# Wo sums on GpSimd, second-wave sums moved, LN steps of neighbouring tiles swapped, w2 ending on four banks

## The chip, the cores and the metric

One core of one Trainium2 chip runs the whole program. The metric is the device time of one execution in microseconds (us), as a median of runs. Inside a profile, times are counted from the span's start.

## The reference, cut to what matters

```
x  : [2048, 1024];  six rows sa, ca, ga, sb, cb, gb = silu(c) @ w_mod
h  = layernorm(x) * (1 + ca) + sa
x1 = x + ga * A(h)                  # attention over 64 segments of 32 tokens, 8 memory tokens, 32 heads of 128
                                    # A ends with o @ Wo  (4096 x 1024)
u  = layernorm(x1) * (1 + cb) + sb
g  = gelu(layernorm(u) @ w1)        # 1024 x 1024, then four channel groups shifted by -1, +1, -2, +2 tokens
v  = u + shifted(g) @ w2
out = x1 + gb * (v + gelu(layernorm(v) @ w3) @ w4)      # 1024 x 3584 and 3584 x 1024
```

## The kernel before

Matrix products are made with one level of a Strassen-like scheme: seven products in place of eight, whose operands are sums of blocks ("sums") and whose results are joined by additions. The work comes in stages, one after the other on TensorE (PE).

**Attention** (about 110 to 773 us). A scheduler orders the instructions of each engine by their place in the program and its own estimates; `keep_order` pins an instruction to its place. Head by head, projections (L649) run between the heads' scores and outputs (L757, L774). VectorE (DVE) joins results (L621), multiplies masks (L763), makes the projection weights' sums (L592) and the sums of Wo, `wo_sum` (L569 to L575): for each of 16 blocks of 256 rows of Wo, four additions of 128x512 16-bit elements, both inputs in SBUF, and a store `WoT_d` (L576) from GpSimd's queue (POOL). Twelve blocks come from tiles `wo2` (two buffers), four from `wstream` (one buffer, shared with loads of the weight check on SyncE's queue, SP). POOL otherwise stores heads (L799) and copies their memory columns (L806 to L808).

**Output projection, two waves** (773 to 990 us). Here and in the next stage the order is written out by hand: `units` is a list of TensorE units of 8 matmuls, and `put(n, f)` places the instructions of `f` behind unit n on every engine. Wave 0 is units 0 to 55 and wave 1 is units 56 to 111. In each wave the seven products come in the order j = 1, 2, 5, 6, 3, 7, 4, each 8 units long (two halves `hf` of four token tiles). `after(j, i)` empties a bank: `snap` copies it on ScalarE (ACT, L946); `fin` adds the snap on DVE (L952) and multiplies by ga (L954). In wave 1, product j=2 is units 64 to 71, j=5 is 72 to 79, j=6 is 80 to 87, j=3 is 88 to 95, j=7 is 96 to 103, j=4 is 104 to 111. A new bank for j=5 needs the `fin` of j=2 done, and j=4 adds onto the bank that j=7's `fin` reads. The eight sums of wave 1, `sums1[hf][k]` (L1002, 128x4096 each), are put at given units.

**Layer norms of the 16 token tiles** run beside the waves and the w1 product. Tile t has a start n in `starts`; at n POOL adds the residual, `C1_x` (L1141, two halves), and issues the stores `x1_d` (L1145); at n+2 DVE takes statistics, `ln_stats` (L1125 to L1129), and POOL makes rstd (L1131, L1132); at n+3 ACT makes u (L1151); at n+5 `C1_mod` on DVE multiplies, adds and takes the second statistics (L1155, L1156, L1125), and POOL makes the second rstd; at n+8 ACT makes z (L1163); at n+9 `C1_out` issues the transposition of z (L1174) and the store of u (L1168), from ACT's queue up to tile 8, from SP's queue behind it. The load of the residual for tile t, `load_x2` (L1118), goes out on POOL's queue at max(n-9, the start of tile t-2).

**w1** (units 112 to 143, L1230): four blocks of 512 tokens of 8 units each. Blocks 2 and 3 need the transposed z of tiles up to 12 and up to 15.

**w2** (`Ba`, L1366): 16 tiles, two banks each, taken in turn from eight banks; DVE adds u (L1368), ACT squares and normalises (L1346, L1353), POOL makes rstd between them.

**w3 and w4** (L1442, L1493; order by hand again): `w3_stage` opens its own bank pools, `bank_b` (four banks), `bank_e` and `bank_d` (two each). In each group of products the copies `snap` (L1407, ACT) of `bank_b` and `bank_d` come before PE adds onto these banks, and `join` (L1450, DVE) and gelu (L1446, ACT) follow.

Of the kernel before, what the change touches and what calls it, by code (L numbers as in the profile page):

```python
# [14 lines left out]
ALU = mybir.AluOpType  # L15
# [14 lines left out]
NTT = S // P  # L30
# [30 lines left out]
def kernel(ctx, tc, A_x, A_mem0, A_Wq, A_Wk, A_Wv, A_Wo, A_seg_len, B_x, B_w1, B_w2, B_w3, B_w4, c, w_mod, out,  # L61
           dbg=None, force_fallback=False, no_fallback=False):
    nc = tc.nc
# [17 lines left out]
    x1_d = dram.tile([S, D], F32, name="x1_d")  # L81
# [70 lines left out]
    def lagged(a_fn, b_fn, ts, lag=2):  # L152
        n = len(ts)
        out_ = []
        for i in range(n + lag):
            fs = []
            if i - lag >= 0:
                fs.append(b_fn(ts[i - lag]))
            if i < n:
                fs.append(a_fn(ts[i]))  # L160
            out_.append(lambda fs=fs: [f() for f in fs])
        return out_

    def p_rows(t):

        if t == 0:
            return [(slice(0, 32), slice(0, 32)), (slice(32, 128), slice(S - 96, S))]
        return [(slice(0, P), slice(32 + P * (t - 1), 32 + P * t))]

    def first_pass(late_hook):  # L170
# [3 lines left out]
        acc_pools = [psA, psA, psX]  # L174
# [71 lines left out]
        keep_order = tc.keep_in_program_order  # L246

        keep_order = tc.keep_in_program_order
# [262 lines left out]
        def f16(ap):  # L511
            return ap.bitcast(F16)

        hA = []
        for p in range(2):
# [3 lines left out]
            s1 = nc.vector.tensor_tensor(S1, A21, A22, ALU.add)  # L519
# [40 lines left out]
        def wo_sum(k, w):  # L560

            B11, B12, B21, B22 = (w[:, b, n] for b in range(2) for n in range(2))
            st = []

            def one():
                st.append(wtp.tile([P, 2, 2, 512], BF16, name="wt"))
                T1, T3, T4, T2 = (f16(st[0][:, b, n]) for b in range(2) for n in range(2))
                st.append((T1, T2, T3, T4))
                keep_order(nc.vector.tensor_tensor(T1, B12, B11, ALU.subtract))  # L569
                nc.vector.tensor_tensor(T2, B22, T1, ALU.subtract)  # L570

            def two():
                T1, T2, T3, T4 = st[1]
                keep_order(nc.vector.tensor_tensor(T3, B22, B12, ALU.subtract))
                nc.vector.tensor_tensor(T4, B21, T2, ALU.subtract)  # L575
                nc.gpsimd.dma_start(WoT_d[:, :, k, :].rearrange("j p c -> p j c"), st[0][:].rearrange("p b n c -> p (b n) c"))  # L576
            return [one, two]

# [356 lines left out]
        x1s = {}  # L935
# [102 lines left out]
        psB = PS.enter_context(tc.tile_pool(name="psB", bufs=4, space=PSUM))  # L1038
# [75 lines left out]
        def load_x2(t):  # L1114
            if t < NTT and t not in xts2:
                xts2[t] = tp.tile([P, D], BF16, name="xt2")
                for rows, toks in p_rows(t):
                    nc.gpsimd.dma_start(xts2[t][rows, :], x2[toks, :])  # L1118
# [16 lines left out]
        def halves_of(ap):  # L1135
            return [ap[:, n * 512:(n + 1) * 512] for n in range(2)]

        def C1_x(t):
            for n in range(2):
                cs = slice(n * 512, (n + 1) * 512)  # L1140
                nc.gpsimd.tensor_tensor(x1s[t, n][:], x1s[t, n][:], xts2[t][:, cs], ALU.add)  # L1141
            for n in range(2):
                cs = slice(n * 512, (n + 1) * 512)
                for rows, toks in p_rows(t):
                    nc.gpsimd.dma_start(x1_d[toks, cs], x1s[t, n][rows, :])  # L1145

        def C1_u(t):
            nmr, rstd = ln[t]
# [4 lines left out]
        def C1_mod(t):  # L1153
            u = us[t]
            nc.vector.tensor_tensor(u[:], u[:], cb1_b[:], ALU.mult)  # L1155
            nc.vector.tensor_tensor(u[:], u[:], sb_b[:], ALU.add)  # L1156
            rstd = bsm.tile([P, 1], F32, name="ln_rstd")
            ln_stats(t, halves_of(u[:]), rstd[:])
# [28 lines left out]
        def next_a(key, hf=None):  # L1187
            def f():
                for x in range(2) if hf is None else (hf,):
                    load_a(1, key, x)  # L1190
            return f
# [47 lines left out]
        def put(n, *fs):  # L1239
            at.setdefault(n, []).extend(fs)  # L1240
# [6 lines left out]
        put(31, next_a((0, 0)))  # L1247
        put(39, next_a((1, 0)))
        put(47, next_a((1, 1)))
        for n, (hf, k) in {58: (0, 0), 60: (1, 0), 62: (0, 1), 64: (1, 1), 65: (0, 2), 67: (1, 2), 76: (0, 3), 78: (1, 3)}.items():  # L1250
            put(n, sums1[hf][k])
        put(79, load_w1)
        put(98, late_slots)
        put(111, open_h1, load_w2)
        starts = [40, 46, 51, 56, 72, 77, 82, 87, 97, 101, 105, 109, 113, 116, 119, 122]
        for t, n in enumerate(starts):
            put(max(n - 9, starts[t - 2] if t > 1 else 0), lambda t=t: load_x2(t))
            put(n, lambda t=t: C1_x(t))
            put(n + 2, lambda t=t: ln_stats(t, [x1s[t, k][:] for k in range(2)], ves[:, t:t + 1]))
            put(n + 3, lambda t=t: C1_u(t))  # L1260
            put(n + 5, lambda t=t: C1_mod(t))
            put(n + 8, lambda t=t: C1_z(t))
            put(n + 9, lambda t=t: C1_out(t))
        put(134, check_b)
# [110 lines left out]
            return lambda: nc.sync.dma_start_transpose(z2s[t // 8][:, :, t % 8 * P:(t % 8 + 1) * P], zs[t][:])  # L1375

        for i, u in enumerate(lagged(Ba, Bb, list(range(NTT)), lag=1)):
            u()
            if i in (4, 8):
                load_upto(ring_ctr[0])  # L1380
            if i == 6:
                zu = w3_sums(0) + [lambda: None] + z_sums(0)
            if 6 <= i < 14 and i != 9:
                keep_order(zu[i - 6]())
# [12 lines left out]
        stA = RF.enter_context(tc.tile_pool(name="x3_sA", bufs=4, side="right"))  # L1397
        st2 = RF.enter_context(tc.tile_pool(name="x3_s2", bufs=2, side="right"))
# [3 lines left out]
        pse = RF.enter_context(tc.tile_pool(name="ps_e", bufs=2, space=PSUM))  # L1402
        psd = RF.enter_context(tc.tile_pool(name="ps_d", bufs=2, space=PSUM))

        def snap(pool, src):
            s = pool.tile([P, 512], F32, name="snap")
            nc.scalar.copy(s[:], src[:])  # L1407
            return s

        def addend_units(pair):  # L1410
# [14 lines left out]
        def w3_stage(pair):  # L1425

            hq = [[hq_p.tile([P, 14, 512], BF16, name=f"hq{a}{f}") for f in range(2)] for a in range(2)]
            A11, A12, S4, A22, S1, S2, S3 = zsum[pair]  # L1430
            add = addend_units(pair)
            for g in range(7):
                n = pair * 11 + g
                load_upto(n + 2)
                B11, B21, B22, T4, T1, T2, T3 = ready[n]
                st = [{} for _ in range(2)]

                def prod(bank, A, B, start):
                    for q in range(2):
                        acc = st[q][bank]  # L1440
                        for k in range(4):
                            nc.tensor.matmul(acc[:], lhsT=B[:, k, q * P:(q + 1) * P], rhs=A[:, k, :], start=(start and k == 0), stop=(k == 3), skip_group_check=True)  # L1442
                        yield q

                def gelu(a, f, q, src):
                    nc.scalar.activation(hq[a][f][:, g * 2 + q, :], src[:], ACT.Gelu_apprx_tanh)  # L1446

                def join(a, f, q, bank, s):
                    t = stm.tile([P, 512], F32, name="join")
                    nc.vector.tensor_tensor(t[:], st[q][bank][:], st[q][s][:], ALU.add)  # L1450
                    gelu(a, f, q, t)

                for q in range(2):
                    st[q]["b"] = psb.tile([P, 512], F32, name="bank_b")
                for q in prod("b", A11, B11, True):
                    st[q]["s1"] = snap(stA, st[q]["b"])
                for q in range(2):
                    st[q]["e"] = pse.tile([P, 512], F32, name="bank_e")
                for q in prod("e", A12, B21, True):
                    join(0, 0, q, "e", "s1")  # L1460
                dve(T4, B21, T2, ALU.subtract)
                for q in range(2):
                    st[q]["d"] = psd.tile([P, 512], F32, name="bank_d")
                for q in prod("d", S1, T1, True):
                    st[q]["s5"] = snap(stA, st[q]["d"])
                for q in prod("b", S2, T2, False):
                    st[q]["s2"] = snap(st2, st[q]["b"])
                for q in prod("b", S3, T3, False):
                    join(1, 1, q, "b", "s5")
                for q in prod("d", S4, B22, False):  # L1470
                    join(0, 1, q, "d", "s2")
                for q in prod("b", A22, T4, False):
                    gelu(1, 0, q, st[q]["b"])
                for u in w3_sums(n + 1) if g < 6 else []:
                    u()
                for u in add[16 * g // 7:16 * (g + 1) // 7]:
                    u()
            return hq
# [805 lines left out]
```

## Time and profile before

| what | value |
|---|---|
| median of 5 runs (lowest to highest) | 1471.76 us (1465.65 to 1473.22) |
| the profiled execution | 1472.42 us |
| its span, first to last instruction | 1470.7 us |
| mean granted TensorE clock | 0.991 |
| busy PE / DVE / ACT / POOL | 1403.7 / 963.7 / 694.0 / 406.5 us |
| PE busy, 110 to 773 us (attention) | 648.83 of 663 us |
| PE busy, 908 to 990 us | 73.23 of 82 us |
| PE busy, 990 to 1057.5 us | 58.33 of 67.5 us |
| PE busy, 1113 to 1130 us | 11.56 of 17 us |

A row of the profile names line, engine, operation and tiles, then the busy time, the mean duration of one in ns, and the idle time of its engine before it with what ended most of it. A row of the waits reads: who waited, for what, us in total, times, the longest. A row of a timeline reads: start in us, duration in us, engine, line, operation, tiles, shapes, count, and in brackets the idle time before and what ended it.

### The profile page before, as it was taken

To read this page: it belongs to the slowest core of one execution; us is meant where nothing else is said; L and a number is where in the kernel's file an instruction comes from. 1 tells how busy PE (TensorE), PEld (TensorE's weight loads), DVE (VectorE), ACT (ScalarE), POOL (GpSimd) and SP (SyncE) were. 2 spreads that over 40 slices of the span, in tenths; PEclk is the share of its full clock that TensorE was granted. 3 is DMA by queue.
4 is the path that set the end of the run, shared out by engine and by line. 5 is a ranking of instruction groups with operands and counts; after the bars stand their busy time and mean duration, and the time that the engine had idled before them with its cause. 6 is when DMAs were issued, how large, how long until landed. Compare 5 with 4: busy or idle time off the path is not lost. (4 is left out here: it accounts for less than half of the span.)

```text
span 1470.7 us, 24781 instructions
## 1 busy us (share of the span) xinstructions
PE 1403.7 (95%) x9126; PEld 741.2 (50%) x9126; DVE 963.7 (66%) x2053; ACT 694.0 (47%) x1479; POOL 406.5 (28%) x611
## 2 busy tenths in 40 slices
PE   6998999999999999999999998988898999999998
PEld 4675555555555555655564443433343444444443
DVE  6627777777776776877753568576355568665684
ACT  2625565564666566666652112325466650046400
POOL 6120010110100100100111045556223663545625
PEclk9999999999999999999999999999999999999999
DMA  9778968987787877788779998888499783477812
GB/s 320 270 237 192 202 143 204 217 180 179 177 202 176 212 166 179 177 181 202 160 176 354 351 334 257 253 192 247 144 279 225 240 267 127 142 226 251 285 45 78
DMA packets 388342, 310.70 MB, mean 211 GB/s; under 512 B 199658, under 2 KB 336874, under 8 KB 384370
## 3 DMA queue, kind: packets, MB, share of 16 engines
q1 hardware_dynamic: 354560, 240.36, 61.5%
q0 software_dynamic: 14976, 49.83, 10.0%
q10 hardware_dynamic: 18674, 18.83, 4.7%
q8 instruction: 73, 1.20, 0.3%
q14 instruction: 59, 0.48, 0.1%
HBM read 199.38 MB, written 59.02 MB: 176 GB/s over the span
## 5 line engine op out<-in xcount | busy, mean ns | idle before, releaser
L987 PE MATMUL acc<-wstream,s 128*128 128x512 f16 (+1 forms) x864 | 191.2, 384 | 12.4 <-DVE snap L952 9.4
L649 PEld LDWEIGHTS <-T 128*128 128x128 f16 x1408 | 130.3, 97 | 118.5 <-issue 2.7
L617 ACT COPY snap<-acc 128x480 f32<-128x480 f32 x264 | 146.0, 566 | 88.1 <-PE acc L649 80.6
L649 PE MATMUL acc<-hh,T 128*128 128x480 bf16 (+1 forms) x704 | 163.2, 367 | 0.0
L649 PE MATMUL acc<-hs,T 128*128 128x480 f16 x704 | 159.1, 366 | 1.5 <-DVE QT L621 1.3
L987 PEld LDWEIGHTS <-s 128*128 128x128 f16 (+1 forms) x864 | 84.9, 99 | 118.3 <-issue 17.8
L799 POOL DMA_DIRECT2D OTw_d<-OT x32 | 24.6, 769 | 407.1 <-DMA OT<-O 343.7
L1442 PEld LDWEIGHTS <-ring 128*128 128x128 f16 (+1 forms) x784 | 76.9, 98 | 104.7 <-issue 13.5
L761 ACT ACTIVATE E<-ps_s 99x495 bf16<-99x495 f32 (+2 forms) x160 | 88.0, 551 | 42.7 <-PE ps_s L757 42.4
L649 PE MATMUL acc<-hh,wq 128*128 128x480 bf16 x464 | 105.6, 366 | 0.8 <-ACT QT L638 0.8
L781 DVE TENSOR_TENSOR O<-ps_o,rin_all 99x384 bf16<-99x384 f32 (+1 forms) x192 | 97.2, 509 | 3.6
L1407 ACT COPY snap<-bank_b 128x512 f32<-128x512 f32 x72 | 41.8, 586 | 105.1 <-PE bank_b L1493 60.7
L621 DVE TENSOR_TENSOR KT<-acc,snap 128x480 bf16<-128x480 f32 x116 | 74.5, 654 | 21.1 <-PE acc L649 15.9
L1493 PEld LDWEIGHTS <-hq 128*128 128x128 bf16 (+1 forms) x560 | 54.7, 98 | 66.1
L774 PE MATMUL ps_o<-V,E 99*128 99x129 bf16 (+1 forms) x704 | 80.9, 220 | 6.2 <-ACT O L779 2.8
L774 PEld LDWEIGHTS <-E 99*128 99x128 bf16 (+1 forms) x704 | 57.2, 98 | 43.4 <-issue 3.3
L1292 DVE TENSOR_TENSOR ring<-ring 128x1024 f16<-128x1024 bf16 (+1 forms) x64 | 75.5, 1199 | 5.3 <-PE bank_b L1493 4.6
L763 DVE TENSOR_TENSOR E<-E,maskB 99x495 bf16<-99x495 bf16 (+1 forms) x128 | 48.1, 376 | 46.3 <-ACT E L761 44.5
L779 ACT ACTIVATE O<-ps_o,rin_all 99x128 bf16<-99x128 f32 x192 | 56.7, 370 | 39.0 <-DVE rin_all L776 36.6
L1493 PE MATMUL bank_b<-ring,hq 128*128 128x512 f16 (+1 forms) x336 | 73.2, 379 | 0.0
L1446 ACT ACTIVATE hq<-join 128x512 bf16<-128x512 f32 x84 | 52.8, 630 | 42.9 <-DVE join L1450 42.7
L1151 ACT ACTIVATE u<-x,ln_nmr,ves 128x512 bf16<-128x512 f32 x32 | 24.3, 806 | 95.4 <-POOL ln_nmr L1132 81.2
(264 smaller groups left out, 2650.8 us busy)
## 6 DMA issues: line engine op xcount, KB each, us to landing
OTw_d<-OT POOLq DMA_DIRECT2D x32, 512.0 KB, 6.3
wstream<-WoT_d SPq DMA_DIRECT2D x16, 1024.0 KB, 10.3
wstream<-in_B_w_dram SPq DMA_DIRECT2D x28, 512.0 KB, 5.0
ring<-in_B_w_dram SPq DMA_DIRECT2D x28, 512.0 KB, 5.9
ring<-in_B_w_dram SPq DMA_DIRECT2D x8, 1792.0 KB, 10.3
s<-OTw_d SPq DMA_DIRECT2D x13, 1024.0 KB, 7.9
wstream<-in_A_Wo_dram SPq DMA_DIRECT2D x11, 1024.0 KB, 14.8
wq<-in_A_Wq_dram SPq DMA_DIRECT2D x16, 512.0 KB, 5.3
```

The source lines that it names most:

```text
L617: nc.scalar.copy(t[:], st[q][bank][:, 0:CH])
L621: nc.vector.tensor_tensor(view(d, i), chunks(st[q][bank]), chunks(st[q][s_]), ALU.add)
L649: nc.tensor.matmul(acc[:, 0:CH], lhsT=B[:, k, :], rhs=A[:, k, :], start=(j in (1, 2, 5) and k == 0), stop=(k == 3), skip_group_check=True)
L761: nc.scalar.activation(E[:rows, 0:o], ps[:rows, 0:o], ACT.Exp, scale=DH ** -0.5)
L774: nc.tensor.matmul(ps[:, i, :], lhsT=state["e", h, t // 5][:k, c:c + P], rhs=V[:k, t, 0:DH + 1], start=True, stop=True)
L779: nc.scalar.mul(O[:rows, t, :], ps[:rows, i, 0:DH], rin[:, i:i + 1])
L781: nc.vector.tensor_tensor(O[:rows, ts[0]:ts[0] + n, :], ps[:rows, 0:n, 0:DH], rin[:, :, None].to_broadcast([rows, n, DH]), ALU.mult)
L987: nc.tensor.matmul(acc[:], lhsT=A[:, k, i * P:(i + 1) * P], rhs=B[:, k, :], start=(j in (1, 2, 5) and hf == 0 and k == 0), stop=(hf == 1 a ...
L1292: return nc.vector.tensor_tensor(dst, a, b, op)
L1442: nc.tensor.matmul(acc[:], lhsT=B[:, k, q * P:(q + 1) * P], rhs=A[:, k, :], start=(start and k == 0), stop=(k == 3), skip_group_check=True)
L1446: nc.scalar.activation(hq[a][f][:, g * 2 + q, :], src[:], ACT.Gelu_apprx_tanh)
L1493: nc.tensor.matmul(acc[:], lhsT=L3[:, k, i * P:(i + 1) * P], rhs=R3[:, k, :], start=(start and k == 0), stop=(k == 13), skip_group_check=True)
```

## The change

1. The 64 additions of `wo_sum` go from DVE to GpSimd, and the `keep_order` on them goes.
2. The sums of wave 1 move from units 58, 60, 62, 64, 65, 67, 76, 78 to units 57, 59, 72, 74, 76, 78, 83, 85.
3. Starts of tiles 1 to 7 move to 45, 50, 55, 60, 76, 81, 86 (from 46, 51, 56, 72, 77, 82, 87); `C1_mod` is put at n+6 in place of n+5, so that the next tile's `C1_x`, or for the last tiles its `ln_stats`, comes ahead of it.
4. The `x1_d` stores of tiles 9 to 15 go from POOL's queue to SP's.
5. The last tiles of w2 take their banks from `psB` (four banks) alone.
6. In the first group of w3, six `snap` copies go from ACT to DVE.

```diff
@@ wo_sum
-                keep_order(nc.vector.tensor_tensor(T1, B12, B11, ALU.subtract))
-                nc.vector.tensor_tensor(T2, B22, T1, ALU.subtract)
+                nc.gpsimd.tensor_tensor(T1, B12, B11, ALU.subtract)
+                nc.gpsimd.tensor_tensor(T2, B22, T1, ALU.subtract)
...
-                keep_order(nc.vector.tensor_tensor(T3, B22, B12, ALU.subtract))
-                nc.vector.tensor_tensor(T4, B21, T2, ALU.subtract)
+                nc.gpsimd.tensor_tensor(T3, B22, B12, ALU.subtract)
+                nc.gpsimd.tensor_tensor(T4, B21, T2, ALU.subtract)
@@ C1_x
-                    nc.gpsimd.dma_start(x1_d[toks, cs], x1s[t, n][rows, :])
+                    (nc.sync if t > 8 else nc.gpsimd).dma_start(x1_d[toks, cs], x1s[t, n][rows, :])
@@ the order by hand
-        for n, (hf, k) in {58: (0, 0), 60: (1, 0), 62: (0, 1), 64: (1, 1), 65: (0, 2), 67: (1, 2), 76: (0, 3), 78: (1, 3)}.items():
+        for n, (hf, k) in {57: (0, 0), 59: (1, 0), 72: (0, 1), 74: (0, 2), 76: (1, 1), 78: (1, 2), 83: (0, 3), 85: (1, 3)}.items():
...
-        starts = [40, 46, 51, 56, 72, 77, 82, 87, 97, 101, 105, 109, 113, 116, 119, 122]
+        starts = [40, 45, 50, 55, 60, 76, 81, 86, 97, 101, 105, 109, 113, 116, 119, 122]
...
-            put(n + 5, lambda t=t: C1_mod(t))
+            put(n + 6, lambda t=t: C1_mod(t))
@@ the loop over w2
+            if i == NTT - 3:
+                acc_pools[:] = [psB]
             u()
@@ w3_stage
-        def snap(pool, src):
+        def snap(pool, src, on_dve=False):
             s = pool.tile([P, 512], F32, name="snap")
-            nc.scalar.copy(s[:], src[:])
+            if on_dve:
+                nc.vector.tensor_copy(s[:], src[:])
+            else:
+                nc.scalar.copy(s[:], src[:])
...
-                    st[q]["s1"] = snap(stA, st[q]["b"])
+                    st[q]["s1"] = snap(stA, st[q]["b"], n == 0)
...
-                    st[q]["s5"] = snap(stA, st[q]["d"])
+                    st[q]["s5"] = snap(stA, st[q]["d"], n == 0)
...
-                    st[q]["s2"] = snap(st2, st[q]["b"])
+                    st[q]["s2"] = snap(st2, st[q]["b"], n == 0)
```

## The prediction

> **What bounds the kernel now.** The page first: PE is busy for 95% of the span, so only its idle time can go, and the question is what ends each idle stretch. The waits of PE, largest first, name the places:
>
> ```profile
> PE small_ps L395 <- DMA wchunk<-in_w_mod_dram: 9.6, 3, 6.3
> PE acc L987 <- DVE snap L952: 9.4, 3, 4.5
> PE bank_b L1442 <- ACT snap L1407: 7.8, 5, 2.2
> PE acc L1230 <- issue: 5.0, 1, 5.0
> PE acc L1230 <- DMA s<-z: 4.2, 1, 4.2
> ```
>
> The first is the start, which the change leaves alone; the other four lie where it edits. The windows by stage give the size: in 82 us of wave 1 PE idles 8.8, in the w1 stage 9.2 of 67.5, at the seam of w2 and w3 5.4 of 17; attention idles 14 of 663.
>
> ```profile
> 110.00:773.00 663.00, 648.83 (x4776) 380.04 (x4775) 482.95 (x1268) 399.30 (x966) 62.94 (x155) 1.00 0.79 185
> ...
> 908.00:990.00 82.00, 73.23 (x323) 32.32 (x323) 55.93 (x107) 19.73 (x26) 43.60 (x61) 0.96 0.84 229
> 990.00:1057.50 67.50, 58.33 (x264) 25.50 (x263) 34.46 (x84) 37.01 (x68) 32.79 (x67) 0.95 0.71 197
> ...
> 1113.00:1130.00 17.00, 11.56 (x40) 4.42 (x40) 3.55 (x10) 11.28 (x18) 3.94 (x10) 0.80 0.87 214
> ```
>
> The clock column (next to last but two) falls below 1 in these windows: after the longer stalls it is granted at 0.5 for 3.4 us, which costs 1.7 us more each time. Then the timelines show the causes. DVE at the first stall, unit 72 (PE idle 907.34 to 911.82):
>
> ```profile
> 902.27 8.89 DVE L1002 TENSOR_TENSOR s<-s,s 128x4096 f16<-128x4096 bf16 x4
> 911.08 0.68 DVE L952 TENSOR_TENSOR snap<-acc,snap 128x512 f32<-128x512 f32 x1
> ...
> 978.36 0.68 DVE L952 TENSOR_TENSOR snap<-acc,snap 128x512 f32<-128x512 f32 x1
> ```
>
> And POOL in the same stretch:
>
> ```profile
> 878.41 0.55 POOL L1131 TENSOR_TENSOR ln_rstd<-ln_mv,mhalf 128x1 f32<-128x1 f32 x1 [4.83 <-DVE ln_mv L1129]
> ...
> 902.38 2.59 POOL L1131 TENSOR_TENSOR ln_rstd<-ln_mv,mhalf 128x1 f32<-128x1 f32 x1 [4.83 <-DVE ln_mv L1129]
> ...
> 967.22 2.26 POOL L1141 TENSOR_TENSOR x<-x,xt 128x512 f32<-128x512 f32 x2 [6.22 <-DMA xt<-in_A_x_dram]
> ```
>
> Four sums stand on DVE ahead of the additions that free unit 72's bank. At 968.79 (unit 104) and 976.69 (unit 107) PE waits again for such additions: once behind statistics that wait for tile 8's residual (POOL idle 6.22), once behind `C1_mod` of tile 8 (975.22 to 978.36). At the third seam ACT still has three tiles of layer norm to do when PE wants the first copies:
>
> ```profile
> 1119.51 1.13 ACT L1346 ACTIVATE z<-x1b,ln_nm 128x1024 bf16<-128x1024 f32 x1
> 1120.64 0.56 ACT L1407 COPY snap<-bank_b 128x512 f32<-128x512 f32 x1
> 1121.94 1.24 ACT L1353 ACTIVATE z<-x1b,ln_nmr,ln_rstd 128x1024 bf16<-128x1024 f32 x1 [0.74 <-POOL ln_nmr L1352]
> 1123.09 0.56 ACT L1407 COPY snap<-bank_b 128x512 f32<-128x512 f32 x1
> ```
>
> **Edit 1, Wo's sums.** Removed from DVE: 64 additions of 0.417 (L569 to L575), 26.7 us. Added on POOL: no row has its 16-bit additions; the nearest, 128x512 in f32 with two inputs in SBUF, take 1.15 (L1141) and 1.28 (L1419), below them only 0.2 to 0.3 for small copies. I take 1.15: 74 us, in 16 bursts of 4.6, on an engine busy 63 of 663. In the built program's order one burst falls every 20 us or so, with a cluster of three near 265 to 295; there the head store L799 behind them (283.67 now) comes about 11 late, still ahead of the 321.7 at which SP turns the head that needs its buffer. SP's load of `wstream` waits for the sums on POOL where it waited for DVE's, with the flips of the heads behind it: first sums before ended at 163, now at about 155 + 4.6 = 160. So no wait replaces the old one. What DVE gains it partly pays back: L954, two inputs in SBUF, takes 0.69 alone and 0.93 to 1.08 beside POOL's L1141; masks, weight sums and row sums (160 x 0.41, 176 x 0.42, 112 x 0.48 = 194 us, 29% of the time) can meet a burst, some three to a burst (29% of 4.6 us, at 0.43 each), 48 x 0.3 = 14 us. DVE, 73% busy here, is not the bound, and PE's 14 us of idle are scattered over some thirty releasers. I take 0, ends -3 and +4 (reordered instructions, among them two of PE's).
>
> The Trainium skill, SBUF — State Buffer, section Who interferes with whom, speaks against this edit: a DVE instruction with two SBUF inputs and a GpSimd one that reads SBUF exclude each other, the second waiting for the whole of the first. The trace agrees in kind: POOL's power takes 0.55, and 2.59 beside a sum of 2.28. By the rule at its worst the 48 meetings cost a whole addition each, an estimate of 55 us of DVE time.
>
> **Edits 2 to 4, wave 1 and w1.** With the four sums behind the additions, DVE's order ahead of unit 72 is: second layer norm of tile 2, sum, statistics, sum, tile 3, tile 4, then the additions. From unit 55's end (879.7): 3.4 + 2.3 + 1.8 + 2.3, a turn over POOL and ACT of 2.4, 3.4 + 1.8, another 2.4, 3.4 = 902.9; unit 68 ends at 902.16, so the bank is free at about 904.3, before 907.34. The X sums that units 72 and 76 read are done by 890. The moved sums run 909 to 918, ahead of units 80 (921) and 84; those at 83 and 85 end by 932, ahead of unit 88 (935). So PE runs on at 1.727 a unit, and unit 103 ends at 962.6 instead of 968.79. `C1_mod` of tile 8 now stands behind its `fin` (1.37): start at 964.0, against 975.22, 11.2 earlier. Tile 8's residual load goes out at about 940 (952.77 before, landing 14.4 later at 967.14): needed by 955, it has 15.
>
> What is late next is the chain of tiles 8 to 15. Before, `C1_mod` starts at 975.22 for tile 8 and 1031.44 for tile 15: 8.0 a tile, a ring of DVE 3.4 + 1.8, POOL 0.83, ACT 1.55 and semaphores. Tiles 8 to 11 keep that order: tile 11 starts at 988, ends at T = 991.4. For tiles 12 to 15 the statistics of t+1 stand ahead of `C1_mod` of t, but POOL's `C1_x` of t+2 stands behind the rstd of t: ring 3.4 + 0.83 + 2.27 + second half of the statistics 1.2 = 7.7, no shorter. Only the last two `C1_mod` run back to back: T + 25.3 = 1016.7 for tile 15, 14.7 ahead of before. Block 3 of w1 then starts at 1041.74 - 14.7 = 1027.0. PE alone would be there at 1017.8, so this chain decides: the stage ends about 14.7 earlier, out of the 25.2 that its stalls cost (6.2 at unit 72, 2.6, 4.1, 5.9, 6.7, clock included). Block 2 waits some 4 us at 1004 for tile 12, which edit 4 delays: SP issues the x1 stores of tile 14 (wait for POOL until 1003.3, then 2 x 0.45) ahead of turning tile 12's z; with no effect on block 3. Edit 4's relief on POOL (1.14 a tile) lies in POOL's idle time: nothing.
>
> The clock's price is from the rows: half clock after 2.56 and 2.40 us of stall as after 4.48. The Trainium skill, TensorE: Matmul & The Clock Gate, Part 1, has an idle window of about 3.4 us ahead of the half clock; by it only the stalls over 3.4 us would pay, and the removable sum here would be 3.4 smaller in w2's seam and 1.7 in wave 1 (estimates).
>
> **Edits 5 and 6, the seam.** Stalls of 0.82 (bank_b behind L1368), 2.20, 1.43, 1.10 and 3.4 us of lost clock: 8.9. Tile 15 now uses banks that bank_b does not get, and DVE, idle for 9.1 here, copies (6 x about 0.68, the price of L952, which reads the same kind of bank): first copy at 1114.6 of before's times, all before PE needs them. Left: gelus still queue behind ACT's last z (1123.2); with three join buffers the fourth join waits for the first gelu (1123.9), and PE's last product for that join, 0.5; copies of 0.68 instead of 0.59, up to 0.4. Gain 8.9 - 0.9 = 8.0. Using four banks for w2's last tile costs nothing: tile 13's are read by 1108, wanted at 1109.3.
>
> **Sum.** 0 - 14.7 - 8.0 = -22.7 from the profiled 1472.42 (span 1470.7 and 1.7 around it), 1449.7; that run is 0.66 above the median, so 1449.
>
> **Rivals.** (a) *Tile 8's residual is late again.* DMA was at 1.07 of its share from 930 to 960. If it lands at 961, unit 104's stall stays and `C1_mod` of tile 8 starts at 970: 5.2 + 8.0 gained, 1458.6. For: the 14.4 us row; against: one tile's traffic now moved out of that stretch. (b) *The seam's stall turns into joins and gelus* (three buffers, ACT behind): half of 8 comes back, 1453. (c) *Slower:* bursts on POOL shut out DVE, and PE follows, 0.5 us for each of 64 additions: +32, 1481. It decides from 0.35 us an addition. For: 2.59 beside 2.28; against: L954's +0.3, DVE's slack. (d) *Block 3's chain shortens with the swap* to DVE's own 5.2 a tile: the w1 stage is then free, 25 + 8, 1439.
>
> **Chances.** Forecast with (b) 0.60, (a) 0.20, (d) 0.07, (c) 0.10, edits cancelling within the noise 0.03. The 80% range takes forecast, (b), (a) with attention's +4: 1441 to 1465. About 0.3% (4.4 us) is what a measurement can tell from no change: faster 0.86, same 0.04, slower 0.10.
>
> **What would show it.** Right: no PE gap at unit 72; `fin` of units 100 to 103 ahead of `C1_mod` of tile 8, which starts 11 ahead of before; a gap remaining ahead of blocks 2 or 3; no L1407 wait at the first w3 group; POOL's additions near 1.15; attention's end within 4 of 773. Wrong: L763 or L592 clearly above 0.41 and attention longer; block 3 without a wait, or as late as before.

## The result, and the profile after

The changed kernel takes 1465.6 us (median of 38 runs, 1459.3 to 1491.8), the kernel before 1472.7 in the runs shared with it (75 runs): a ratio of 0.9953, 95% interval 0.9937 to 0.9968. It is faster by about 7 us, where 23 were forecast; 1465.6 lies just outside the range. Some executions of either kernel run at a lower mean clock and take over 1.5% longer; the ratios leave them out, and the profile of run e8 below is one of them, so that only its time is used.

The profiled execution took 1464.76, with a span of 1463.0. The stages follow one another on PE, so the times between the first matmuls of the stages say where the 7.6 us between the two profiles came from (in us; the last column is the span of w2's first to w3's first matmul, part of the fourth):

| run | until first scores | attention | output projection and w1 | w2 and first w3 | w4 to last matmul | (w2 alone) |
|---|---|---|---|---|---|---|
| before | 106.8 | 666.3 | 284.4 | 148.7 | 257.5 | (56.3) |
| after | 104.5 | 673.2 | 269.5 | 151.4 | 257.5 | (55.3) |
| after - before | -2.3 | +6.9 | -14.9 | +2.7 | 0 | |
| forecast | 0 | 0 | -14.7 | -8.0 | 0 | |

So the middle term held to 0.2 us (how far by luck is said at the end); attention, forecast to stay, grew, and the seam of w2 and w3, forecast to shrink, grew too. The start is not touched by the change: over all profiles here it lies between 104.4 and 106.8.

The windows by stage of the changed kernel, over attention, the second wave, w1, and the seam of w2 and w3 (columns: window, length, then busy time and count of PE, its weight loads, DVE, ACT, POOL, then clock, DMA share, GB/s):

```profile
110.00:773.00 663.00, 644.83 (x4700) 375.37 (x4699) 481.22 (x1194) 394.79 (x951) 138.70 (x216) 1.00 0.76 182
908.00:990.00 82.00, 82.00 (x381) 37.12 (x380) 68.93 (x116) 24.28 (x31) 46.74 (x65) 1.00 0.84 250
990.00:1047.00 57.00, 48.08 (x212) 20.81 (x211) 26.45 (x69) 30.97 (x61) 23.48 (x44) 0.91 0.69 193
1102.50:1123.50 21.00, 12.09 (x46) 4.87 (x45) 8.39 (x17) 9.33 (x13) 5.97 (x13) 0.76 1.05 229
```

The second wave has no idle time left (8.8 before). In attention PE idles 18.2 of 663 in place of 14.2, and DVE is as busy as before (481.2 against 483.0) although 64 additions have gone to POOL. The seam idles 8.9 and its clock is at 0.76. The waits of PE name the heads of these losses (the first is what is left ahead of blocks 2 and 3 of w1):

```profile
PE acc L1230 <- DMA s<-z: 8.9, 2, 6.5
PE bank_b L1447 <- DVE snap L1410: 8.6, 1, 8.6
...
PE ps_o L774 <- DVE O L781: 3.1, 3, 1.6
...
PE acc L649 <- DVE QT L621: 2.9, 3, 2.4
```

The second is new: one wait of 8.6, for the very copies (L1410) that were moved to DVE. DVE's timeline there:

```profile
1104.85 0.69 DVE L1410 COPY snap<-bank_b 128x512 f32<-128x512 f32 x1
...
1105.51 0.68 DVE L1410 COPY snap<-bank_b 128x512 f32<-128x512 f32 x1
1114.88 1.29 DVE L1455 TENSOR_TENSOR join<-bank_e,snap 128x512 f32<-128x512 f32 x2 [8.68 <-ACT z L1353]
...
1116.68 1.28 DVE L1410 COPY snap<-bank_d 128x512 f32<-128x512 f32 x2
1117.88 1.28 DVE L1410 COPY snap<-bank_b 128x512 f32<-128x512 f32 x2
```

The first two copies are as early as forecast. Then DVE stands 8.68 us at the first join, which waits for ACT's last z, and the four other copies, which PE needs, stand behind it in DVE's order.

In attention, one burst of POOL's additions (275.51 to 281.53) met these rows of DVE:

```profile
276.22 0.42 DVE L593 TENSOR_TENSOR T<-wk,T 128x512 f16<-128x512 bf16 x1
276.55 1.38 DVE L272 SCALAR_TENSOR_TENSOR row_a<-row_w,sc,row_a 128x256 f32<-128x256 bf16 x1
277.86 1.37 DVE L595 TENSOR_TENSOR T<-wq,T 128x512 f16<-128x512 bf16 x1
279.15 1.37 DVE L272 SCALAR_TENSOR_TENSOR row_a<-row_w,sc,row_a 128x256 f32<-128x256 bf16 x1
280.45 0.17 DVE L776 RECIPROCAL rin_all<-ps_o 104x3 f32<-104x3 f32 x1
280.54 1.27 DVE L763 TENSOR_TENSOR E<-E,maskB 99x495 bf16<-99x495 bf16 x1
```

The four that take 1.27 to 1.38 here take 0.4 to 0.5 elsewhere, DVE falls 3.6 us behind, and PE waits 2.44 at 282.10 for a join that comes after them (DVE QT L621).

### The profile page after: what moved, and what is told of

Its sections match the earlier page's. It is cut to its first block, busy times and chain, and to the rows that moved or that the text cites. A ratio compares the mean times of both kernels' runs of the same rounds, so it can differ in the third digit from the quotient of the medians.

```text
span 1463.0 us, 24767 instructions
## 1 busy us (share of the span) xinstructions
PE 1399.9 (96%) x9126; PEld 740.3 (51%) x9126; DVE 975.9 (67%) x1995; ACT 692.7 (47%) x1473; POOL 478.2 (33%) x661
## 4 chain that ended last, share of the span: by engine, by line
PE 72%; DVE 10%; DMA 9%; ACT 4%; issue 3%; POOL 1%; SPq 1%; ACTq 0%; DVEq 0%; POOLq 0%
PE acc L649 27%; PE acc L987 9%; PE bank_b L1498 7%; PE bank_b L1447 6%; PE bank_d L1447 3%; DMA s<-OTw_d 3%; PE acc L323 3%; PE bank_e L1498 2%; PE bank_d L1498 2%; PE acc L333 2%; PE ps_o L774 2%; PE ps_s L757 2%; PE acc L1366 1%; PE bank_e L1447 1%; DVE row_a L272 1%
## 5 line engine op out<-in xcount | busy, mean ns | idle before, releaser
L987 PE MATMUL acc<-wstream,s 128*128 128x512 f16 (+1 forms) x864 | 187.3, 379 | 1.6 <-DMA wstream<-in_A_Wo_dram 1.0
L781 DVE TENSOR_TENSOR O<-ps_o,rin_all 99x384 bf16<-99x384 f32 (+1 forms) x192 | 97.2, 509 | 3.9
L621 DVE TENSOR_TENSOR KT<-acc,snap 128x480 bf16<-128x480 f32 x116 | 74.3, 653 | 22.6 <-PE acc L649 15.8
L763 DVE TENSOR_TENSOR E<-E,maskB 99x495 bf16<-99x495 bf16 (+1 forms) x128 | 52.7, 412 | 48.4 <-ACT E L761 46.5
L1292 DVE TENSOR_TENSOR ring<-ring 128x1024 f16<-128x1024 bf16 (+1 forms) x64 | 79.9, 1268 | 5.3 <-PE bank_b L1498 4.9
L621 DVE TENSOR_TENSOR VT<-acc,snap 128x480 bf16<-128x480 f32 x90 | 58.0, 651 | 22.8 <-PE acc L649 15.8
```

The costliest lines, as they stand in the source:

```text
L621: nc.vector.tensor_tensor(view(d, i), chunks(st[q][bank]), chunks(st[q][s_]), ALU.add)
L781: nc.vector.tensor_tensor(O[:rows, ts[0]:ts[0] + n, :], ps[:rows, 0:n, 0:DH], rin[:, :, None].to_broadcast([rows, n, DH]), ALU.mult)
L987: nc.tensor.matmul(acc[:], lhsT=A[:, k, i * P:(i + 1) * P], rhs=B[:, k, :], start=(j in (1, 2, 5) and hf == 0 and k == 0), stop=(hf == 1 a ...
L1292: return nc.vector.tensor_tensor(dst, a, b, op)
```

## The experiments

The theories: **D**, POOL's additions hold up DVE in attention, and PE behind it; **A**, the copies stand behind a join that waits for the last z; **G**, the join waits because of the memory under it. The stages of all runs (us, first matmul to first matmul) and the ratio to before:

| run | attention | projection, w1 | w2, first w3 | w4 on | ratio (95%) |
|---|---|---|---|---|---|
| e1 copies on ACT | 672.7 | 270.7 | 149.4 | 257.5 | 0.9924 (0.9897 to 0.9952) |
| e2 joins behind copies | 673.0 | 272.4 | 147.4 | 257.5 | 0.9910 (0.9879 to 0.9941) |
| e3 sums on DVE | 665.4 | 270.3 | 149.4 | 257.5 | 0.9902 (0.9868 to 0.9936) |
| e4 edit 1 alone | 674.0 | 281.0 | 153.7 | 257.5 | 1.0072 (1.0039 to 1.0106) |
| e5 pools reordered | 668.1 | 271.1 | 145.4 | 267.9 | 0.9964 (0.9929 to 1.0000) |
| e6 e5, sums on DVE | 666.9 | 271.3 | 144.2 | 270.4 | 0.9917 (0.9891 to 0.9944) |
| e7 edits 2 to 4 alone | 666.3 | 270.6 | 149.7 | 257.5 | 0.9902 (0.9864 to 0.9940) |
| e8 edits 5, 6 alone | - | - | - | - | 1.0016 (0.9984 to 1.0047) |
| e9 sums cut to 8 columns | 665.8 | 270.6 | 155.2 | 257.8 | 0.9925 (0.9889 to 0.9961) |
| e10 e6, earlier addends | 666.4 | 271.4 | 143.0 | 266.3 | 0.9911 (0.9884 to 0.9938) |
| e11 copies for sums | 666.1 | 270.7 | 149.1 | 257.5 | 0.9869 (0.9819 to 0.9919) |
| e12 no swap, no edit 4 | 669.2 | 282.3 | 157.0 | 257.5 | 1.0026 (0.9994 to 1.0058) |
| e13 e6, four buffers | 666.8 | 275.6 | 143.1 | 260.8 | 0.9836 (0.9799 to 0.9873) |
| e14 no edit 4 | 671.6 | 270.8 | 151.7 | 257.5 | 0.9925 (0.9889 to 0.9957) |
| e15 no edit 5 | 671.7 | 269.7 | 149.9 | 257.5 | 0.9923 (0.9889 to 0.9957) |

Single profiles of one stage's code differ by some us, and the intervals of the ratios reach about 0.3% to either side: rows that differ by less are not told apart.

### Edit 1: Wo's sums

e3 puts the additions back on DVE in the changed kernel (the first of the four is shown); e4 is the reverse edit in the kernel before:

```diff
-                nc.gpsimd.tensor_tensor(T1, B12, B11, ALU.subtract)
+                keep_order(nc.vector.tensor_tensor(T1, B12, B11, ALU.subtract))
...
```

> The changed kernel with edit 1 undone: Wo's sums on DVE, with their pinned order. Theory D (sums on GpSimd cost the attention 5 to 7 us, as the two profiles say: matmuls 2.27 ahead at 65 us, 4.68 behind at 773, 3.01 behind from unit 24 on): PE is level with its start offset at the end of attention, time 1459 to 1461. Rival E (that loss is one of this execution, or of a few reordered instructions, not of the edit; edit 1 costs nothing): time 1464 to 1467 and a loss of 4 or more in attention again.

> The kernel before with edit 1 alone. Theory D: attention 5 to 7 us longer, 1.7 of it given back in wave 0, time 1476 to 1479; DVE's mask products (L763) and weight sums (L592 to L595) at means of 0.41 to 0.51 in place of 0.38 to 0.43. Rival E: within 2 us of before, 1471 to 1474. Rival F (DVE's 26.7 us of relief help): 1467 to 1470.

e3: 1459.1 us, attention 665.4. e4: 1481.2, attention 674.0, in a kernel that is otherwise before's. Theory D holds, E and F fall. Over all profiles, attention takes 668.1 to 674.0 with full sums on POOL (eight of them, mean 671.7) and 665.4 to 666.9 with none there.

e9 and e11 ask what about the additions does it. e9 cuts them to 8 of 512 columns and stores Wo's blocks as they are, e11 copies one operand; so both leave Wo's sums out of the result. Both leave every instruction of PE, DVE, ACT and SP in the changed kernel's order (again the first of four):

```diff
-                nc.gpsimd.tensor_tensor(T1, B12, B11, ALU.subtract)
+                nc.gpsimd.tensor_tensor(T1[:, 0:8], B12[:, 0:8], B11[:, 0:8], ALU.subtract)   # e9
+                nc.gpsimd.tensor_copy(T1, B12)                                                # e11
...
```

> The changed kernel with the 64 additions cut to 8 of their 512 columns, the store taking Wo's blocks as they are (so most of the sums of Wo are left out); the order on PE, DVE, ACT and SP is the changed kernel's, to the instruction. Theory D (GpSimd's additions hold up DVE's instructions that read two SBUF operands, and PE waits behind them): attention, from its first scores to the first matmul of the output projection, falls from 673.2 to 665 to 667 us, DVE's mask products and weight sums go back to means of 0.38 and 0.42, the whole to 1457 to 1459. Rival K (the reordered instructions of DVE and PE cost it, or the lost pinning): 671 to 673, the whole within 2 of the changed kernel's 1465.6.

> The changed kernel with each of the 64 additions on GpSimd replaced by a copy of its first operand (128x512, 16 bit; the sums of Wo are left out); order on PE, DVE, ACT and SP unchanged. If it takes two SBUF reads on both sides to shut DVE out, attention falls to 665 to 668 us (673.2 in the changed kernel), DVE's rows stay at 0.38 and 0.42. If any GpSimd work on SBUF does it: 669 to 673, in proportion to the copies' length.

e9: 665.8 of attention, so rival K falls: the reordering costs nothing that shows, the additions do. (The whole, 1462.8, is above the 1457 to 1459 expected; in its profile w2 alone took 60.7 us in place of 55.3, see the end of the point by point.) Groups of DVE in attention, changed kernel first, then e9:

```profile
L763 DVE TENSOR_TENSOR E<-E,maskB 99x495 bf16<-99x495 bf16 x124 | 51.3, 414 | 48.4 <-ACT E L761 46.5
L594 DVE TENSOR_TENSOR T<-wk 128x512 f16<-128x512 bf16 x28 | 14.0, 501 | 0.0
```

```profile
L763 DVE TENSOR_TENSOR E<-E,maskB 99x495 bf16<-99x495 bf16 x124 | 46.7, 377 | 49.5 <-ACT E L761 47.6
L594 DVE TENSOR_TENSOR T<-wk 128x512 f16<-128x512 bf16 x28 | 11.7, 416 | 0.0
```

By the windows, DVE is busy 464.8 us in e9's attention and 485.4 in the changed kernel's: the bursts cost it 20.6. The same sums on DVE (e3) make it 483.2, so what the edit took off DVE was 18.4. It gave back all of that, and at places where PE waits. DVE's relief by itself is worth nothing here: 665.8 with next to no sums, 665.4 with all of them on DVE.

e11's copies take 0.64 to 0.70 each in place of 1.22 to 1.30. DVE's attention rises to 469.7, a quarter of the 20.6 for half of POOL's time, with L594 at 0.445; PE feels nothing, 666.1. So copies of one operand come with a DVE that is held up too, but less than in proportion to their length; whether one operand or the shorter bursts make the difference was not separated.

### Edits 5 and 6: the seam

e1 undoes edit 6, e15 undoes edit 5, e8 makes both in the kernel before:

> The changed kernel with edit 6 undone: the six copies of w3's first group are on ACT again, edit 5 stays. After the change, PE's matmuls run 10.25 us ahead of before at the end of w1 and 7.53 ahead behind the seam, so the seam lost 2.7. Theory A (the copies on DVE stand behind the first join, which waits for ACT's last z): with the copies on ACT the seam goes back to about before's form, stalls of 2.2, 1.4 and 1.1 and some 3.4 us of half clock's worth; PE is ahead by 10 to 10.8 behind the seam; time 1462 to 1463, about 3 us less than the changed kernel. Rival B (edit 5 is the cause: w2's last tiles on four banks come late, or open the banks to w3 too early): the lead stays at 7 to 8, time 1465 to 1466.

> The changed kernel with edit 5 alone undone (all eight banks to the end of w2; the copies stay on DVE). If edit 5 takes nothing and brings little: PE waits 0.4 to 1 at w3's first matmul for the bank that tile 15's additions empty, then as long as in the changed kernel for the copies; w2's first to w4's first matmul 149 to 152 (151.4, 149.4), the whole 1464 to 1467. If the four banks cost (waits of 6 in w2 in two runs where u came late): 144 to 147, 1458 to 1461.

> The kernel before with edits 5 and 6 alone. Theory A and G (the copies wait with the joins for ACT's last z): w2's first to w4's first matmul 148 to 152 us (148.7 before), time 1472 to 1476, no gain. Rival (the seam's loss after the change comes from the earlier start of w2 there, not from edits 5 and 6; with before's start they save their 8): 141 to 143, time 1464 to 1466.

e1: 1462.3; the seam takes 149.4, PE waiting 3.2, 0.6 and 1.1 for copies on ACT. With the copies on DVE it took 151.4, 149.4, 149.1, 151.7 and 149.9 in five profiles of the same w3. So moving them costs 0 to 2 us and gains nothing; A's direction holds, B falls. e15: 1466.8; 0.92 of wait at the first bank, then 5.9 for the copies: edit 5 takes and brings nothing that shows. e8: 1477.5, no gain at before's start of w2 either, so its rival falls.

e2 and e5 ask why the copies wait. e2 places the first two joins behind them:

```diff
                 for q in prod("e", A12, B21, True):
-                    join(0, 0, q, "e", "s1")
+                    if n:
+                        join(0, 0, q, "e", "s1")
...
                     st[q]["s2"] = snap(st2, st[q]["b"], n == 0)
+                for q in range(0 if n else 2):
+                    join(0, 0, q, "e", "s1")
```

> The changed kernel with one order changed: in w3's first group the two joins of bank_e come behind the copies s5 and s2 on DVE, in place of ahead of them; nothing is left out. Theory A (DVE's queue stops at a join that waits for the last z, the copies behind it would not wait): the gap of 8.55 at 1110 goes, and with it the half clock from 1112.8 to 1123.05 (5.1 us); PE is ahead of before by 10.25 + 8.9 - 0 to 2, 17 to 19 behind the seam; time 1452 to 1455. Rival C (whatever DVE writes in the new pools waits for the last z, the copies too, or gelus on ACT behind z take over as the bound): the gap stays at 5 or more, time 1461 to 1466.

Half right: the gap fell from 8.55 to 4.46, not to zero, and the time to 1461.6, in C's range. (The 5.1 for the clock was too much: of the 10.24 us at half clock only 4.4 lay in PE's work, 2.2 lost.) DVE's timeline shows which copy waits now:

```profile
1110.71 0.69 DVE L1410 COPY snap<-bank_d 128x512 f32<-128x512 f32 x1 [0.17 <-PE bank_d L1447]
1111.57 0.69 DVE L1410 COPY snap<-bank_d 128x512 f32<-128x512 f32 x1 [0.17 <-PE bank_d L1447]
1116.98 1.29 DVE L1410 COPY snap<-bank_b 128x512 f32<-128x512 f32 x2 [4.72 <-ACT z L1353]
```

The copies s5 (`stA`) run at once; s2 (`st2`) waits for the last z itself, though it reads nothing of it. What `st2` and the joins' `stm` have in common is their memory: they are laid over w2's small layer-norm tiles, which z reads as bias and scale. e5 opens the pools in another order:

```diff
-        hq_p = RF.enter_context(tc.tile_pool(name="x3_h", bufs=1, side="right"))
-        ring_pools[1] = RF.enter_context(tc.tile_pool(name="x3_rB", bufs=2, side="right"))
         stA = RF.enter_context(tc.tile_pool(name="x3_sA", bufs=4, side="right"))
         st2 = RF.enter_context(tc.tile_pool(name="x3_s2", bufs=2, side="right"))
         stm = RF.enter_context(tc.tile_pool(name="x3_sm", bufs=3, side="right"))
+        ring_pools[1] = RF.enter_context(tc.tile_pool(name="x3_rB", bufs=2, side="right"))
+        hq_p = RF.enter_context(tc.tile_pool(name="x3_h", bufs=1, side="right"))
```

> The changed kernel, with the pools of w3 opened in another order: the copies' and joins' buffers (x3_sA, x3_s2, x3_sm) first, the gelu's output last, so that copies and joins no longer lie on the memory of w2's small layer-norm tiles; nothing else differs. Theory G (the first joins, and the copies s2 of the run with late joins, waited because x3_sm and x3_s2 overlap the 20 KB of ln tiles that ACT's last z reads: join at 120800 to 126944 and s2 from 126944, ln tiles up to 127268): DVE's copies and joins run as PE fills the banks, the gap of 8.55 at the seam goes to under 1.5 (the fourth join waits for the first gelu behind the last z), no or one window of half clock; from w2's first to w4's first matmul 139 to 143 us in place of 151.4 (149.4 in the run with sums on DVE); time 1452 to 1457. Rival H (gelus on ACT behind the last z, or the weights' ring in its new place, take over): 147 to 151, time 1460 to 1466.

> The changed kernel with the pools of w3 in that order and edit 1 undone (Wo's sums on DVE). By theories D and G together: 1465.6 - 6.5 (the run with sums on DVE) - 8 to 12 = 1447 to 1451. By D and H: 1457 to 1460.

G holds for the mechanism: with other memory under the same copies and joins, and no other edit, the wait for z is gone. DVE's timeline of e5:

```profile
1103.53 1.28 DVE L1455 TENSOR_TENSOR join<-bank_e,snap 128x512 f32<-128x512 f32 x2
1104.73 0.68 DVE L1292 TENSOR_TENSOR ring<-ring 128x1024 f16<-128x1024 bf16 x1
1105.33 1.28 DVE L1410 COPY snap<-bank_d 128x512 f32<-128x512 f32 x2
1106.66 0.69 DVE L1410 COPY snap<-bank_b 128x512 f32<-128x512 f32 x1
...
1113.59 0.69 DVE L1455 TENSOR_TENSOR join<-bank_b,snap 128x512 f32<-128x512 f32 x1 [4.44 <-ACT hq L1451]
```

No copy or join waits for z, only the fourth join for a gelu, as the prediction had it (PE 2.46, where 0.5 was forecast). The seam takes 145.4 and 144.2, a gain of 4 to 7, less than expected. But the whole comes to 1466.7 and 1461.3: w4 takes 10 to 13 us more. Its cause, in e5's POOL, DVE and PE:

```profile
1190.61 4.88 POOL L1424 TENSOR_TENSOR xb<-xb,gb_b 128x512 f32<-128x512 f32 x1 [4.15 <-DMA xb<-x1b_d]
1195.57 4.79 POOL L1425 TENSOR_TENSOR x<-xb,x 128x512 f32<-128x512 f32 x1
```

```profile
1190.47 3.89 DVE L1292 TENSOR_TENSOR zs<-hq,hq 128x7168 f16<-128x7168 bf16 x1 [1.74 <-ACT hq L1451]
1194.40 4.84 DVE L1292 TENSOR_TENSOR hq<-hq,hq 128x7168 f16<-128x7168 bf16 x1
1213.40 3.89 DVE L1292 TENSOR_TENSOR ring<-ring 128x7168 f16<-128x7168 bf16 x1 [14.16 <-DMA ring<-in_B_w_dram]
```

```profile
PE bank_e L1498 <- DVE join L1520: 4.1, 1, 4.1
PE bank_e L1498 <- DVE hq L1292: 2.8, 1, 2.8
```

POOL's operations for the output's addend (x1 + gb * v, added in w4; normally 1.27 each) ran beside DVE's sums of 128x7168 (3.89 alone). Each waited for one sum and ended 1.1 behind it; the second sum, behind the first of them, took 4.84. SP, whose next loads wait for the addends' buffers, stood from 1191 to 1200, and the last loads of w4's weights behind them (the `ring` buffers) went out at 1204.4, 15 us behind w4's first matmul; the third sum waited 14.16 for them, and PE for the joins behind it. In the changed kernel the same load goes out at 1198.3, 0.3 ahead of it: that stream had been covered by the seam's stall. e10 spreads the addends over six groups of w3, e13 gives them four buffers in place of two:

```diff
-                for u in add[16 * g // 7:16 * (g + 1) // 7]:
+                for u in add[16 * g // 6:16 * (g + 1) // 6]:                                       # e10
-        rsq = RF.enter_context(tc.tile_pool(name="x3_rq", bufs=2, side="right"))
+        rsq = RF.enter_context(tc.tile_pool(name="x3_rq", bufs=4, side="right"))                   # e13
```

> The kernel with the pools of w3 reordered and Wo's sums on DVE, and with one thing more: the 16 addend units of a pair are spread over the first six groups of w3 instead of seven. In the run without that, w4 took 10.4 us more than elsewhere (267.9 against 257.5): the last addend units on POOL ran beside DVE's 128x7168 sums (4.9 us an addition in place of 1.27), SP waited for their buffers, and the first load of w4's ring behind them went out at 1204.4, to land 8.9 later. Theory L (that queue is all there is to it): w4 back to 257 to 259, the whole 1446 to 1451. Rival M (the new places of the pools delay the ring in another way, or DMA is the bound): 264 to 268 again, the whole 1457 to 1462.

> The kernel with the pools of w3 reordered and Wo's sums on DVE, with addend buffers (x3_rq) four deep in place of two. So far the seam's gain of 5 to 8 us came back as a loss of 9 to 10 in w4, whose ring loads stand in SP's queue behind the addend loads. Theory P (SP stands at addend loads that wait for their two buffers, 1191 to 1200 in the run with reordered pools): with four buffers the last two ring loads of w4 go out within 3 us of w4's first matmul (15 behind it without), w4 takes 257 to 259 us in place of 267.9, the whole 1446 to 1452. Theory Q (the transfers themselves, ring and addends together, take that long from the end of layer norm on): the loads go out as late as before, or land later, w4 264 to 268, the whole 1458 to 1462.

e10: 1460.7, w4 still 266.3; L falls in that form. The last ring loads went out at 1190.8, 5.7 behind w4's first matmul, and landed as late as 1206.4. e13: 1455.9, w4 260.8, the last load at 1192.2, level with w4's first matmul. That is P: the addend loads are all out by 1177.9, the last ring load waits only for PE's last product of w3, and PE waits nowhere in the first w4. w4 is 2 to 3 and the whole 4 us above what was expected; 2.7 of that are three more waits for copies on ACT in the second w3, inside the last column. (The profiled execution is the slowest of e13's six, with 275.6 for projection and w1, 4 above e6 and e10.) e13 has the lowest ratio of all versions that compute everything, 0.9836.

### Edits 2 to 4: the waves and w1

e7 makes them in the kernel before; e12 undoes the swap (`C1_mod` back at n+5) and edit 4 in the changed kernel, e14 edit 4 alone:

> The kernel before with edits 2 to 4 alone. If the prediction's working of wave 1 and w1 holds: from the first matmul of the output projection to w2's first 269 to 271 us (284.4 before, 269.5 after), no wait at units 72, 104 and 107, waits of 2 to 3 and 6 to 8 ahead of blocks 2 and 3 of w1; time 1457 to 1460. Rival (the gain there needs edit 1 too, since the run with edit 1 alone already had 281.0 in place of 284.4): 273 to 275, time 1462 to 1464.

> The changed kernel with the swap of neighbouring tiles' steps (C1_mod back at n+5) and edit 4 (x1 stores back on POOL's queue) undone; the places of the sums and the starts stay. The prediction's working says that neither shortens the chain of tiles but for the last two C1_mod back to back: from the output projection's first matmul to w2's first 269.5 + 2 to 4, 271 to 274 us; the whole 1467 to 1470. Rival N (the chain does need the swap or the relief of POOL): 276 to 284, the whole 1472 to 1480. Rival O (the swap costs, since block 3 waits 6.5 with it): 265 to 268, the whole 1461 to 1464.

> The changed kernel with edit 4 alone undone (x1 stores of tiles 9 to 15 on POOL's queue). The run without swap and edit 4 lost 12.8 us between the output projection's start and w2 (282.3 against 269.5). If that is the swap's, as the order says (without it C1_mod of tiles 3 and 4 and their waits of 2.4 us stand ahead of unit 72's additions: 6.0 us of wait there), this run stays at 269 to 271 and the whole at 1464 to 1467. If it is POOL's relief: 277 to 283, 1474 to 1479.

e7: 1458.6, 270.6 for the stage, no wait at units 72, 104 and 107, waits of 2.5 and 7.6 ahead of blocks 2 and 3: the working holds, without edit 1. e12: 1478.7 and 282.3, so N holds and my expectation was wrong by 10 us. Its waits in wave 1 and w1:

```profile
PE acc L987 <- DVE snap L952: 7.3, 2, 6.0
PE acc L1230 <- DMA s<-z: 5.9, 1, 5.9
PE acc L1230 <- issue: 4.8, 2, 4.6
```

e14: 1466.6 and 270.8, so edit 4 is worth about 1 at most, and the rest of the 12.8 us that e12 lost is the swap's, by itself or together with edit 4.

## Why the prediction was right or wrong, point by point

**Edits 2 to 4: right in place and mechanism; the size is in part luck.** PE waits nowhere in units 72 to 111. From unit 56 on the changed kernel lies 3.0 us behind before; less these, `C1_mod` of tile 8 starts at 964.0 (forecast 964.0), that of tile 15 at 1014.5 (1016.7), block 3 at 1028.6 (1027.0):

```profile
966.98 0.69 DVE L1155 TENSOR_TENSOR u<-u,cb_b 128x1024 bf16<-128x1024 bf16 x1
...
1017.52 0.68 DVE L1155 TENSOR_TENSOR u<-u,cb_b 128x1024 bf16<-128x1024 bf16 x1
```

The chain of 7.4 to 7.8 a tile decides, and rivals (a) and (d) fall. But of the stage's 14.9 us, 1.7 were gained at the start of wave 0, ahead of these edits (4.7 behind before at its first matmul, 3.0 from unit 24 on), so they brought 13.3. Two errors of the working also met: tile 15's `C1_mod` came 2.2 earlier than forecast, and from there to block 3 took 14.1 us in place of before's 10.3. SP issued loads of w3's weights (1022.32 to 1024.99) ahead of tile 15's transposition, whose z was ready at 1023.42, and the issue of that (1025.10) took 3.63 in place of 1.88. The order ahead of unit 72 that the prediction worked out ran tiles 3 and 4 back to back; what it did not say, and e12 showed, is that this is the swap's doing: without it the stage keeps 2 of its 15 us.

**Edits 5 and 6: wrong; the failing step is "DVE, idle for 9.1 here, copies".** Those 9.11 us of before were not free time. The row carried its reason:

```profile
1123.21 1.29 DVE L1450 TENSOR_TENSOR join<-bank_e,snap 128x512 f32<-128x512 f32 x2 [9.11 <-ACT z L1353]
```

DVE stood at an instruction that waited, and whatever comes behind it in DVE's order waits too. The working counted the wait as room, for it looked at when the copies' banks were full and not at what stands ahead of the copies. Rival (b) knew that joins wait, but for gelus and at half the price. The same row hinted at the true cause, memory shared with w2's small tiles: the joins read nothing that z makes. The copies were priced rightly (0.68); what the seam brought in place of 8.0 was a loss of 2.7 against before, with one wait of 8.6.

**Edit 1: wrong in the term's size; the failing step is that DVE "is not the bound".** POOL's price was right (1.15 forecast; means of 1.22 to 1.30 with meetings), the first bursts' places too. DVE's payback, forecast at 14, was 20.6, and the relief was 18.4, not 26.7 (a row's duration overlaps its neighbour's by about 0.09, which makes 26.7 into 21; the rest is not accounted for). The chief slip is that slack is a mean over 663 us: within a burst DVE loses 3 to 4 us at once, and a join that PE waits for stands behind. Rival (c) had the mechanism but a price of 0.5 an addition; it was 5.4 / 64 = 0.08, and in the changed kernel's own profile 6.9 / 64 = 0.11.

The rule that the prediction took from the Trainium skill, SBUF — State Buffer, section Who interferes with whom, is borne out in kind: rows of DVE with two operands in SBUF go from 0.42 to 1.37 beside POOL's 1.15, and POOL's 1.27 to 4.88 beside DVE's 3.89, while rows that read PSUM stay (L781 0.510 in both kernels, L621 0.654 and 0.653). Its worst case, 55 us of DVE time, was too high by 34.

**The sum.** With the measured terms, -2.3 + 6.9 - 14.9 + 2.7 = -7.6, which is the difference of the last matmuls (1463.69 and 1456.13). Of the 15 us by which the forecast missed (7.6 against 22.7), the seam has 10.7, attention 6.9, and the start goes against them with 2.3. Edits 2 to 4 alone (e7) reach a ratio of 0.9902, the whole change 0.9953, and the whole change without edit 1 (e3) 0.9902 again: edit 1 gave back about half of what the others had gained. Two slips of the working changed nothing in the sum: its five stall costs add up to 25.5, not 25.2, and of the stalls of 2.56 and 2.40 only the second was followed by half clock (at 979.87), as its own terms 2.6 and 4.1 have it.

**Left open.** w2 alone took 55.3 us in most profiles, but 60.6 and 60.7 in e4's and e9's and 64.0 in e12's (59.0 in e7's, where the next wait is 3.4). There the sum `zs` that is mixed into DVE's work in w2 waited 8.5 to 11.1 us for the transposed z2a (3.3 in before, 3.2 in after), with w2's additions behind it: again an instruction that waits at the head of DVE's order. What delays that transposition was not tried.

## What to carry to other kernels

An engine's idle time ahead of an instruction that waits is no room for new work: ask what stands at the head of its queue and what that waits for, and where it waits for something that it doesn't read, look at whose memory it will overwrite. Work moved to an engine that holds up another's instructions, as POOL does DVE's here, costs where the two meet, in bursts, so a mean share of busy time does not price it. When a stall is removed, name the transfers that it covered: here they were the next bound, and it took the buffers behind them to keep the gain.

## What the runs showed of the hardware

- DVE and POOL hold each other up for whole instructions, also over long ones: POOL's operation of 1.27 took 4.88 beside a DVE sum of 3.89, and the next sum, 3.89 alone, took 4.84 behind it (e5).
- Within the program the lower clock is granted in stretches of 3.41, 6.83 or 10.24 us: 3.41 after a gap of PE of 4.46 (e2), 6.83 after 5.89 (e15), 10.24 after 8.55 (the changed kernel). The gap does not set the length: in e1, 10.24 came with gaps of 3.20, 0.59 and 1.09 at the same seam. The gap of 2.44 in attention brought half clock in e1 (at 285.3) and e4 (at 284.3) and none in the changed kernel, e2 and e14, at the same place in the program.
- Half clock can fall within the gap that brings it: of the 10.24 us at the changed kernel's seam 5.8 cost nothing, since PE stood still.
